# A fused convolution and two feed-forward layers: hand-made semaphores and fixed buffers in place of the framework's

## The chip, the cores and the metric

The kernel runs on one core of a Trainium2 chip. The metric is device microseconds of one execution. The core has five engines that each take their instructions from a queue of their own, in order: TensorE (PE, whose weight loads are shown as PEld), VectorE (DVE), ScalarE (ACT), GpSimd (POOL) and SyncE (SP, which issues nearly all DMAs). They wait for one another through semaphores.

## The reference, cut to what matters

```python
def reference(x, weight, w_in1, w_out1, w_in2, w_out2, a, b):      # x: 2 x 4096 x 192, float32
    w = softmax(weight, axis=-1)                                    # 8 heads x 7 taps
    x = causal_depthwise_conv(x, w)                                 # each head's 24 channels share 7 taps
    x = x.reshape(8192, 192)
    h = x @ w_in1                                                   # 192 -> 2048
    x = (h * clip(h + 3, 0, 6) / 6) @ w_out1                        # 2048 -> 192
    h = x @ w_in2
    P = a[0] + a[1] * h + a[2] * h**2 + a[3] * h**3
    Q = 1 + abs(b[0]) * abs(h) + abs(b[1]) * h**2
    return (P / (Q + 1e-6)) @ w_out2
```

## The kernel before, in words

The 8192 tokens are cut into 16 blocks of 512 (the last one into two units of 256 each, so 17 units). Every unit goes through both layers in 16 steps of 128 hidden channels (8 double steps for a half unit). Each float32 product is made of products of rounded parts: a value is split into a high part (ACT: `hi1`, `hi2`) and the rest (POOL: `lo1`, `lo2`). So one step of a layer costs TensorE five matmuls into a PSUM bank (`mm1`, `mm3`; line 504) and five into two accumulators (`product_out`, lines 518 to 523). Twenty matmuls of 512 columns make one step of both layers.

Between the matmuls of layer 2 a value goes along a chain through all the other engines (class `L2`, lines 610 to 704): ACT `A`, `t1` and `S` read the bank; DVE `t2` (line 656) and `t3` (line 668) build the numerator in the tile T; POOL `q` (line 662) the denominator in S; ACT `R` and `RR` (line 677) write the inverse square into the bank; DVE `w` (line 682) reads S and the bank and writes S; DVE `p2` (line 686) reads T and the bank and writes the bank; DVE `G` (line 691) reads S and the bank and writes T; then come `hi2`, `lo2` and the matmuls. Layer 1 is shorter: ACT `u` (line 562), DVE `g` (line 567), `hi1`, `lo1`.

At the start, 12 `warm` matmuls run on zeros, POOL clears six half tiles (`zero_low`, line 467), DVE makes the softmax of the taps in 18 tiny operations on 8 partitions (`band_ops`, lines 266 to 281), whose result `line` goes to DRAM and comes back as the convolution's band matrix (lines 952, 287), and the weights, which arrive as 64-bit words, are decoded in tiles (`mag_w`, `bound_w`, `bits_w`, `hi_w`, `lo_w`, lines 347 to 410).

The order of the work is written by the kernel itself. `Issue.at` (line 84) records every operation with a planned time, an engine, a duration, the function that emits it, and the keys that it reads and writes (`r`, `w`). `Issue.graph` (line 88) turns the keys into edges, each with a flag `end`: true if the later operation must wait for the earlier one's end, false if it only has to be issued after it. Keys need not be real buffers: `zero_low` reads the key `("line", 0)` (line 949), which the softmax operations write (line 951), though the two touch no common memory. A ring (`rings`, line 221) says how many buffers a key's name has. `Issue.order` (line 126) simulates the five engines with these edges and gives one list. The list is then emitted under the framework's manual schedule (line 967), and the framework, which sees the buffers of every single instruction, allocates the buffers of the pools and inserts all semaphore waits and signals itself. The two lines in the graph that matter here:

```python
        pred[written[key]] = True                                   # 113: reads or rewrites what p wrote
        pred[p] = pred.get(p, False) or ops[p][2] != eng            # 116: overwrites what p read
```

So if an operation overwrites what an earlier one on the same engine read (`p2` the bank that `w` read), the flag is false.

Of the kernel before, what the change touches and what calls it, by code (L numbers as in the profile page):

```python
# [62 lines left out]

class Issue:
# [23 lines left out]
    def graph(self):  # L88
        ops = sorted(self.ops, key=lambda o: o[:2])
        succ = [[] for _ in ops]  # L90
        need = [0] * len(ops)
        users, written, read, turn, gone = {}, {}, {}, {}, set()
        for k, (_, _, eng, ns, _, _, r, w, _, _) in enumerate(ops):
            pred = {}
            assert all(key in written for key in r), r
            for key in (*r, *w):
                assert key not in gone, key
                ring = self.rings.get(key[0])
                if key not in users:
# [21 lines left out]
            for p, end in pred.items():  # L121
                succ[p].append((k, end))
                need[k] += 1
        return ops, succ, need

    def order(self):
# [29 lines left out]
        while best:  # L156
# [4 lines left out]
            out.append((f, args))  # L161
# [17 lines left out]


@with_exitstack
def conv_moe_moe_kernel(ctx: ExitStack, tc: tile.TileContext, x, weight, w_in1, w_out1, w_in2, w_out2,
# [7 lines left out]
    nc = tc.nc  # L190
# [17 lines left out]
    p1 = ctx.enter_context(tc.tile_pool(name="p1", bufs=2))  # L208
    p2 = ctx.enter_context(tc.tile_pool(name="p2", bufs=2))
    xp = ctx.enter_context(tc.tile_pool(name="xp", bufs=3))  # L210
    xt = ctx.enter_context(tc.tile_pool(name="xt", bufs=3))
    xs = ctx.enter_context(tc.tile_pool(name="xs", bufs=1))
    sg = ctx.enter_context(tc.tile_pool(name="sg", bufs=4))
    sgm = ctx.enter_context(tc.tile_pool(name="sgm", bufs=5))
    xl = ctx.enter_context(tc.tile_pool(name="xl", bufs=2))
# [3 lines left out]
    bank = [ps.tile([128, C], F32, name=f"bank{k}") for k in range(4)]  # L219

# [31 lines left out]
    def warm():  # L252

        if not spare:
            spare.append(pa.tile([128, C], F32, tag="acc11", name="warm"))
# [63 lines left out]
    def load_w(kind, l, c):  # L319
# [3 lines left out]
        t = sg.tile([128, 512 * words], I32, tag="raw", name="raw")  # L323
# [17 lines left out]
    def mag_w(key, k):  # L341
# [4 lines left out]
        r[2] = sgm.tile([128, 512], F32, tag="m", name="m")[:, 0:n] if boxed(key) else r[3]  # L346
# [72 lines left out]
    def zero_x(b):  # L419
        xn[b] = xl.tile([128, NS, DM], F32, tag="xn", name="xn")  # L420
        nc.vector.memset(xn[b][0:KT - 1, 0, :], 0.0)

    def load_x(b):
# [3 lines left out]
        if b not in xn:  # L427
            xn[b] = xl.tile([128, NS, DM], F32, tag="xn", name="xn")
# [19 lines left out]
    def conv_ev(b, half):  # L448
        if b not in x1n:
            x1n[b] = xs.tile([SEG, NS, DM], F32, tag="x1n", name="x1n")  # L450
# [18 lines left out]
    def x1_hi(b, part):  # L469

        tag = "x1b" if part else "x1ah"
        if (b, tag) not in x1:
            x1[b, tag] = xp.tile([128, C], F32R, tag=tag, name=tag)
# [3 lines left out]
    def x1_lo(b, part):  # L477
        c = x1p[b, part]
        if part == 0:
            x1[b, "x1al"] = t = xp.tile([128, C], F32R, tag="x1al", name="x1al")  # L480
# [25 lines left out]
    def product_out(l, u, i, lo):  # L506

        n = units[u][2]
        if (l, u) not in acc:
            k = 1 if l or u == 1 else 0  # L510
            acc[l, u] = [pa.tile([128, C], F32, tag=f"acc{k}{j}", name=f"acc{l}{j}")[:, 0:n] for j in range(2)]
# [13 lines left out]
    def site1(b, i):  # L525

        if b == 1:
            return p2, ("T", "g2h", "g2l"), 1
        return p1, ("u", "g1h", "g1l"), 0
# [15 lines left out]
    def place2(b, i, j):  # L545
        tag = site2(b, i)[0][j]
        p = dict(u=p1, g1h=p1, g1l=p1, m=sgm).get(tag, p2)
        t = p.tile([128, C], F32R if tag[0] == "g" else F32, tag=tag, name=tag)
        return t.bitcast(F32R) if tag == "m" and j > 2 else t

    class L1:
        @staticmethod
        def mm1(b, i):
            h1[b, i] = bank[site1(b, i)[2]]
# [4 lines left out]
        def u(b, i):  # L559
            p, tags, _ = site1(b, i)  # L560
            v1[b, i] = p.tile([128, C], F32, tag=tags[0], name=tags[0])
# [8 lines left out]
        def hi1(b, i):  # L570
            p, tags, _ = site1(b, i)
            gh = p.tile([128, C], F32R, tag=tags[1], name=tags[1])
# [4 lines left out]
        def lo1(b, i):  # L577
            p, tags, _ = site1(b, i)
            gl = p.tile([128, C], F32R, tag=tags[2], name=tags[2])
# [3 lines left out]
    def x2_op(b, nm):  # L583
# [3 lines left out]
        if (b, tag) not in x2:  # L587
            n = units[b][2]
            x2[b, tag] = (low2[b % 3] if tag == "x2ml" else xt.tile([128, C], F32R, tag=tag, name=tag))[:, 0:n]
# [421 lines left out]
```

## Time and profile before

| what | value |
|---|---|
| median of three runs | 1277.68 us (1277.4 to 1277.82) |
| profiled execution | span 1275.4 us from the first to the last instruction |
| granted TensorE clock | 0.999 of full speed over the span |
| busy share | PE 98%, PEld 81%, DVE 89%, ACT 92%, POOL 87% |
| instructions | 18529, waits and DMA issues among them |
| DMA | 28.6 MB, most of it in the first 100 us |

The profiled execution's own time outside its span isn't shown; the median of the runs is 2.3 us above the span, and that is taken as what lies around it. A matmul's end in the records is modelled and overlaps the next one's start, so an idle time of TensorE shorter than some 0.15 us is not seen in the busy time.

### The profile page before, as it was taken

To read this page: it belongs to the slowest core of one execution; us is meant where nothing else is said; L and a number is where in the kernel's file an instruction comes from. 1 tells how busy PE (TensorE), PEld (TensorE's weight loads), DVE (VectorE), ACT (ScalarE), POOL (GpSimd) and SP (SyncE) were. 2 spreads that over 40 slices of the span, in tenths; PEclk is the share of its full clock that TensorE was granted. 3 is DMA by queue.
4 is the path that set the end of the run, shared out by engine and by line. 5 is a ranking of instruction groups with operands and counts; after the bars stand their busy time and mean duration, and the time that the engine had idled before them with its cause. 6 is when DMAs were issued, how large, how long until landed. Compare 5 with 4: busy or idle time off the path is not lost.

```text
span 1275.4 us, 18529 instructions
## 1 busy us (share of the span) xinstructions
PE 1252.6 (98%) x5952; PEld 1031.3 (81%) x5952; DVE 1139.4 (89%) x1824; ACT 1169.1 (92%) x2168; POOL 1116.0 (87%) x954
## 2 busy tenths in 40 slices
PE   8999999999999999999999999999999999999997
PEld 5667888888888888888888888888888888888886
DVE  6998889898898989889899898988988889899998
ACT  5778999999999999999999999999989999999997
POOL 3898898888989899888898898989889898899986
PEclk9999999999999999999999999999999999999999
DMA  5441000000000000000000001000010000000000
GB/s 167 145 147 38 16 1 17 12 13 17 5 15 11 13 16 13 16 2 12 16 13 16 14 1 25 5 16 13 1 29 2 9 5 1 13 1 13 1 13 13
DMA packets 60440, 28.60 MB, mean 22 GB/s; under 512 B 41276, under 2 KB 57272, under 8 KB 60344
## 3 DMA queue, kind: packets, MB, share of 16 engines
q1 hardware_dynamic: 60184, 27.28, 8.5%
q8 instruction: 46, 0.75, 0.3%
q14 instruction: 50, 0.41, 0.1%
q10 hardware_dynamic: 160, 0.16, 0.0%
HBM read 21.13 MB, written 6.30 MB: 22 GB/s over the span
## 4 chain that ended last, share of the span: by engine, by line
PE 80%; DVE 11%; ACT 5%; issue 2%; POOL 2%; DMA 0%; SPq 0%; DVEq 0%; ACTq 0%; POOLq 0%
PE bank L504 38%; PE acc L518 8%; PE acc L521 8%; PE acc L523 8%; PE acc L522 8%; PE acc L519 8%; PE bank L445 2%; DVE bank L686 1%; PE bank L460 1%; DVE u L567 1%; DVE bank L373 1%; DVE T L691 1%; DVE S L682 1%; ACT bank L677 1%; DVE T L656 1%
## 5 line engine op out<-in xcount | busy, mean ns | idle before, releaser
L580 POOL TENSOR_TENSOR g1l<-u,g1h 128x512 fp32r<-128x512 f32 x240 | 311.5, 1298 | 38.3 <-ACT g1h L574 8.2
L662 POOL TENSOR_TENSOR S<-A,S 128x512 f32<-128x512 f32 x169 | 219.2, 1297 | 43.2 <-ACT S L648 34.4
L704 POOL TENSOR_TENSOR g2l<-T,g2h 128x512 fp32r<-128x512 f32 x169 | 219.4, 1299 | 3.1 <-ACT g2h L696 3.0
L504 PE MATMUL bank<-low,B 128*128 128x512 f32 (+1 forms) x544 | 205.2, 377 | 0.0
L567 DVE SCALAR_TENSOR_TENSOR u<-u,bank 128x512 f32<-128x512 f32 x240 | 163.8, 682 | 33.2 <-ACT u L562 31.9
L574 ACT ACTIVATE g1h<-u 128x512 fp32r<-128x512 f32 x240 | 152.1, 634 | 3.6 <-DVE u L567 3.2
L562 ACT ACTIVATE u<-bank 128x512 f32<-128x512 f32 x240 | 143.9, 600 | 8.1 <-PE bank L504 4.0
L682 DVE SCALAR_TENSOR_TENSOR S<-S,bank 128x512 f32<-128x512 f32 x169 | 115.3, 682 | 32.1 <-ACT bank L677 26.9
L662 POOL TENSOR_TENSOR ST<-m,ST 128x512 f32<-128x512 f32 x85 | 110.3, 1298 | 26.6 <-ACT ST L648 20.6
L656 DVE SCALAR_TENSOR_TENSOR T<-T,coef,bank 128x512 f32<-128x512 f32 x169 | 125.2, 741 | 7.8 <-ACT T L641 7.0
L668 DVE SCALAR_TENSOR_TENSOR T<-T,coef,bank 128x512 f32<-128x512 f32 x169 | 125.4, 742 | 1.7
L686 DVE SCALAR_TENSOR_TENSOR bank<-T,coef,bank 128x512 f32<-128x512 f32 x169 | 126.3, 747 | 0.0
L504 PEld LDWEIGHTS bank<-low,B 128*128 128x128 f32 x544 | 102.3, 188 | 19.2
L696 ACT ACTIVATE g2h<-T 128x512 fp32r<-128x512 f32 x169 | 107.4, 635 | 10.8 <-DVE T L691 7.3
L641 ACT ACTIVATE T<-bank,coef 128x512 f32<-128x512 f32 x169 | 116.0, 686 | 0.5 <-POOL g2l L704 0.2
L691 DVE SCALAR_TENSOR_TENSOR T<-S,bank 128x512 f32<-128x512 f32 x169 | 114.9, 680 | 1.5
L673 ACT ACTIVATE A<-S 128x512 f32<-128x512 f32 x169 | 107.3, 635 | 8.8 <-POOL S L662 8.2
L504 PE MATMUL bank<-x1ah,Ah 128*128 128x512 f32 (+1 forms) x272 | 106.8, 393 | 6.4 <-DVE u L567 3.0
L704 POOL TENSOR_TENSOR m<-ST,m 128x512 fp32r<-128x512 f32 x85 | 110.3, 1298 | 1.8 <-ACT m L696 1.8
L504 PE MATMUL bank<-x2ah,Ah 128*128 128x512 f32 (+1 forms) x272 | 104.5, 384 | 3.8 <-DVE T L691 2.2
L677 ACT ACTIVATE bank<-A 128x512 f32<-128x512 f32 x169 | 102.7, 608 | 1.4 <-DVE T L668 0.4
L504 PE MATMUL bank<-x2m,B 128*128 128x512 f32 (+1 forms) x272 | 102.7, 378 | 0.6 <-ACT x2m L598 0.6
(161 smaller groups left out, 3886.1 us busy)
## 6 DMA issues: line engine op xcount, KB each, us to landing
raw<-in_moe_w_out_dram SPq DMA_DIRECT2D x16, 384.0 KB, 3.2
xn<-in_x_dram SPq DMA_DIRECT2D x14, 384.0 KB, 3.5
raw<-in_moe_w_in_dram SPq DMA_DIRECT2D x16, 256.0 KB, 3.0
out_dram<-oac SPq DMA_DIRECT2D x60, 64.0 KB, 2.0
raw<-in_moe_w_in_dram SPq DMA_DIRECT2D x16, 128.0 KB, 3.5
out_dram<-osb SPq DMA_DIRECT2D x15, 128.0 KB, 2.0
xn<-in_x_dram SPq DMA_DIRECT2D x16, 96.0 KB, 3.3
xn<-in_x_dram SPq DMA_DIRECT2D x2, 288.0 KB, 6.5
```

The costliest lines, as they stand in the source:

```text
L504: nc.tensor.matmul(out=dst[:, cs], lhsT=w[nm][:, fs], rhs=m, start=(k == 0), stop=(k == 4))
L562: act(out=v1[b, i], in_=h1[b, i], func=ACTF.Relu, scale=1.0 / 6.0, bias=0.5)
L567: stt(out=t, in0=t, scalar=1.0, in1=h1.pop((b, i)), op0=ALU.min, op1=ALU.mult)
L574: act(out=gh, in_=v1[b, i], func=ACTF.Copy)
L580: nc.gpsimd.tensor_tensor(out=gl, in0=v1.pop((b, i)), in1=f32(g1[b, i][0]), op=ALU.subtract)
L656: stt(out=d["T"], in0=d["T"], scalar=coef[:, 2:3], in1=h2[b, i], op0=ALU.add, op1=ALU.mult)
L662: (nc.gpsimd if k else nc.vector).tensor_tensor(out=d["S"], in0=d["A"], in1=d["S"], op=ALU.add if k == 1 else ALU.mult)
L668: stt(out=d["T"], in0=d["T"], scalar=coef[:, 1:2], in1=h2[b, i], op0=ALU.add, op1=ALU.mult)
L682: stt(out=d["S"], in0=d["S"], scalar=c1, in1=h2[b, i], op0=ALU.add, op1=ALU.mult)
L686: stt(out=h2[b, i], in0=v2[b, i]["T"], scalar=coef[:, 0:1], in1=h2[b, i], op0=ALU.add, op1=ALU.mult)
L691: stt(out=d["T"], in0=d["S"], scalar=2.0, in1=h2.pop((b, i)), op0=ALU.subtract, op1=ALU.mult)
L704: e.tensor_tensor(out=gl, in0=v2.pop((b, i))["T"], in1=f32(gh), op=ALU.subtract)
```

## The change

The operations and the planner's constants stay as they are. The framework's waits are turned off by a critical section, and the kernel makes its own. `graph` now also keeps, for every operation, the list `after` of the operations behind which it has to wait; `emit` goes through the planned list, collects for each operation the marks of the operations in `after`, and adds marks for an operation that touches a PSUM bank or accumulator after another engine did, and for some neighbours on POOL. `Signals.run` drops the marks that the engine is known to have seen already, directly or through another engine's signal, puts the last wait that is left on the operation's first instruction and the others into wait instructions of their own, and lets the operation's last instruction add one to its engine's semaphore. A DMA operation takes the next of 24 lanes. `Slots` gives fixed buffers, by turns. At the end `close` lets SP wait for all lanes.

```diff
+class Slots:
+    def __init__(self, pool, **tags):
+        self.line = {tag: [pool.tile(shape, dt, name=f"{tag}_{k}") for k in range(n)] for tag, (n, shape, dt) in tags.items()}
+        self.turn = dict.fromkeys(self.line, 0)
...
+class Signals:
+    def __init__(self, tc, core, lanes):
+        self.engine = dict(P=core.tensor, A=core.scalar, V=core.vector, G=core.gpsimd, S=core.sync)
+        self.sem = {e: tc.alloc_semaphore(f"done{e}") for e in "PAVG"}
+        self.sem.update({k: tc.alloc_semaphore(f"lane{k}") for k in range(lanes)})
...
+    def waits(self, e, marks):
+        want = {}
+        for sem, n in marks:
+            if self.known[e].get(sem, 0) < n:
+                want[sem] = max(n, want.get(sem, 0))
+        out = [(s, n) for s, n in want.items()
+               if not any(t != s and self.seen[t, m].get(s, 0) >= n for t, m in want.items())]
...
+    def run(self, e, dma, marks, f, args, made, signal):
...
+        todo = self.waits(e, marks)
+        f_ = lambda: f(*args)
+        keep = todo[-1:] if f.__name__ not in self.EMPTY else []
+        for s, n in todo[:len(todo) - len(keep)]:
+            self.engine[e].wait_ge(self.sem[s], n)
+        f_()
+        for s, n in keep:
+            made[0]._wait_ge(self.sem[s], n)
...
+        elif signal:
+            made[-1].then_inc(self.sem[e], 1)
+            self.count[e] += 1
+            mark = e, self.count[e]
...
+    def close(self):
+        for lane in range(self.lanes):
+            if self.known["S"].get(lane, 0) < self.count[lane]:
+                self.engine["S"].wait_ge(self.sem[lane], self.count[lane])
...
     def graph(self):
+        self.after = after = [[] for _ in ops]
+        cross = lambda p, k: ops[p][2] != ops[k][2] or ops[p][8] is not None
...
                             for p in users[line[-ring]]:
-                                pred[p] = pred.get(p, False) or ops[p][2] != eng
+                                pred[p] = pred.get(p) or cross(p, k)
                             gone.add(line[-ring])
                         if line:
-                            pred.setdefault(users[line[-1]][0], False)
+                            pred.setdefault(users[line[-1]][0], None)
...
             for key in w:
                 for p in read.pop(key, ()):
-                    pred[p] = pred.get(p, False) or ops[p][2] != eng
+                    pred[p] = pred.get(p) or cross(p, k)
...
             for p, end in pred.items():
+                if end is not None:
+                    after[k].append(p)
...
+    def emit(self, tc, core, made):
+        out = self.order()
...
+        self.signals = signals = Signals(tc, core, 24)
+        inner = lambda p, k: ops[p][2] == ops[k][2] == "P"
+        wanted = {p for k, line in enumerate(self.after) for p in line if not inner(p, k)}
...
+        held = {}
+        for k in out:
+            e = ops[k][2]
+            for key in (*ops[k][6], *ops[k][7]):
+                if key[0][:4] == "bank" or key[0][:3] == "acc":
+                    line = held.setdefault(key[0], {})
+                    for x, p in line.items():
+                        if x != e and p != k:
+                            self.after[k].append(p)
+                            wanted.add(p)
+                    line[e] = k
+        for k in out:
+            _, _, e, _, f, args, _, _, after, _ = ops[k]
+            marks = [mark[p] for p in self.after[k] if not inner(p, k) and mark[p]]
+            mark[k] = signals.run(e, after is not None and f.__name__ != "x1_raw", marks, f, args, made, k in wanted)
+        signals.close()
...
-    with tc.manual_schedule():
-        for f, a in plan.order():
-            f(*a)
+    with tc.tile_critical():
+        plan.emit(tc, core, nc.made)
```

The rest of the diff replaces every `pool.tile(...)` by the matching `slots.tile(...)`, with the same number of buffers.

## Rows read from the trace of the kernel before

**Rows 1.** Busy time by stretch: start:end, length, each engine's busy us, clock, DMA share, GB/s.
```profile
0.00:50.00 50.00, 44.46 (x179) 29.52 (x179) 38.50 (x90) 30.49 (x64) 28.87 (x36) 1.00 0.57 165
50.00:100.00 50.00, 46.85 (x205) 35.05 (x205) 47.40 (x99) 39.44 (x85) 45.05 (x45) 1.00 0.49 146
...
400.00:800.00 400.00, 399.88 (x1838) 330.84 (x1837) 358.74 (x553) 377.36 (x693) 356.77 (x299) 1.00 0.06 13
```

**Rows 2.** The chain of waits from 150 to 1200 us, shares by line.
```profile
by line: PE bank L504 44.6%; PE acc L518 8.9%; PE acc L521 8.9%; PE acc L519 8.8%; PE acc L523 8.8%; PE acc L522 8.8%; PE bank L445 2.0%; PE bank L460 1.2%; DVE bank L686 0.8%; DVE T L691 0.6%; DVE T L656 0.6%; issue 0.6%; DVE S L682 0.6%; 
```

**Rows 3.** Timeline of the start, 0 to 30 us: start us, us, engine, line, operation.
```profile
1.31 2.91 POOL L467 MEMSET low<- 64x512 f32 x6
2.21 0.15 DVE L266 TENSOR_REDUCE one<-tap 8x1 f32<-8x7 f32 x1 [0.89 <-DMA tap<-in_weight_dram]
6.21 0.22 DVE L281 TENSOR_SCALAR line<-tmp,one 8x7 f32<-8x7 f32 x1
6.91 0.70 DVE L352 TENSOR_SCALAR bank<-bank 128x512 f32<-128x512 f32 x1 [0.48 <-ACT bank L347]
7.64 0.70 DVE L370 TENSOR_SCALAR bank<-bank 128x512 int32<-128x512 int32 x1
10.88 0.92 SPq L287 DMA_DIRECT2D band<-line_d  x2
14.79 2.04 PE L445 MATMUL bank<-xn,band 128*122 128x120 f32 x16 [0.97 <-DVE bank L373]
```

**Rows 4.** DVE's timeline: the first and last of 217 neighbours L682, L686.
```profile
121.72 0.68 DVE L682 SCALAR_TENSOR_TENSOR S<-S,bank 128x512 f32<-128x512 f32 x1
122.32 0.75 DVE L686 SCALAR_TENSOR_TENSOR bank<-T,coef,bank 128x512 f32<-128x512 f32 x1
...
1266.43 0.69 DVE L682 SCALAR_TENSOR_TENSOR u<-u,bank 128x512 f32<-128x512 f32 x1
1267.04 0.75 DVE L686 SCALAR_TENSOR_TENSOR bank<-u,coef,bank 128x512 f32<-128x512 f32 x1
```

**Rows 5.** What DVE waited for: us in total, times, longest us.
```profile
DVE u L567 <- ACT u L562: 31.9, 64, 1.0
DVE S L682 <- ACT bank L677: 26.9, 48, 1.3
...
DVE ST L682 <- ACT bank L677: 14.6, 35, 1.2
```

**Rows 6.** PE and DVE at an accumulator's reuse, 351.5 to 353.2 us.
```profile
351.96 0.69 DVE L602 TENSOR_TENSOR low<-acc,low 64x512 fp32r<-64x512 f32 x1
352.01 0.39 PE L521 MATMUL acc<-g1h,O 128*128 128x512 f32 x1
...
352.80 0.47 PE L523 MATMUL acc<-g1h,O 128*128 128x512 f32 x1 [0.17 <-DVE low L602]
```

**Rows 7.** Separate wait instructions before line 682: count, ns min/median/max, first and last start.
```profile
L682 DVEq EVENT_SEMAPHORE  x104: 21/21/21, 121.4 to 1266.4; - x104
```

**Rows 8.** ACT L677 and the DVE L682 that waits for it, twice.
```profile
245.74 0.60 ACT L677 ACTIVATE bank<-m 128x512 f32<-128x512 f32 x1
...
246.45 0.69 DVE L682 SCALAR_TENSOR_TENSOR ST<-ST,bank 128x512 f32<-128x512 f32 x1 [0.81 <-ACT bank L677]
...
605.92 0.59 ACT L677 ACTIVATE bank<-m 128x512 f32<-128x512 f32 x1
...
606.54 0.69 DVE L682 SCALAR_TENSOR_TENSOR ST<-ST,bank 128x512 f32<-128x512 f32 x1 [0.48 <-ACT bank L677]
```

**Rows 9.** Who waited for DVE's L691 and L567: us in total, times.
```profile
  PEld bank L504: 7.5, 16
...
  PEld bank L504: 14.6, 26
```

**Rows 10.** SP's own waits, at the end of the kernel (L1006).
```profile
SPq L1006 <- DMA out_dram<-osb: 1.5, 1, 1.5
...
SPq L1006 <- PEq L1006: 0.6, 2, 0.4
```

More of the change, by code (lines that the diff above doesn't have):

```diff
@@ L61, with __init__, __getattr__, call @@
 )
+class Engine:
+    def __init__(self, engine, made):
+        self.engine, self.made = engine, made
+    def __getattr__(self, name):
+        f = getattr(self.engine, name)
+        def call(*args, **kw):
+            i = f(*args, **kw)
+            self.made.append(i)
+            return i
+        return call
+class Recorder:
+    def __init__(self, core):
+        self.made = []
+        for name in ("tensor", "vector", "scalar", "gpsimd", "sync"):
+            setattr(self, name, Engine(getattr(core, name), self.made))
@@ L160, in order @@
             _, _, _, ns, f, args, _, _, after, _ = ops[k]
-            out.append((f, args))
+            out.append(k)
             free[e] = start + ns
@@ L178, in order @@
         return out
+    def emit(self, tc, core, made):
+        out = self.order()
+        ops = sorted(self.ops, key=lambda o: o[:2])
+        self.signals = signals = Signals(tc, core, 24)
+        mark = {}
+        inner = lambda p, k: ops[p][2] == ops[k][2] == "P"
+        wanted = {p for k, line in enumerate(self.after) for p in line if not inner(p, k)}
+        odd = lambda k: ops[k][4].__name__ == "zero_low" or ops[k][4].__name__ == "lo_w" and ops[k][5][-1] > 0
+        pool = [k for k in out if ops[k][2] == "G"]
+        for p, k in zip(pool, pool[1:]):
+            if odd(p) != odd(k):
+                self.after[k].append(p)
[8 more added lines that the diff above has]
+                        if x != e and p != k:
+                            self.after[k].append(p)
+                            wanted.add(p)
+                    line[e] = k
[4 more added lines that the diff above has]
+        signals.close()
 @with_exitstack
@@ L345, in mag_w @@
         r.append(bank[k][:, 0:n])
-        r[2] = sgm.tile([128, 512], F32, tag="m", name="m")[:, 0:n] if boxed(key) else r[3]
+        r[2] = slots.tile("m")[:, 0:n] if boxed(key) else r[3]
         act(out=r[2] if CLAMP[side_of(key)] else r[3], in_=f32(t.rearrange("p (n w) -> p n w", w=2)[:, :, 1]), func=ACTF.Abs)
@@ L510, in product_out @@
             k = 1 if l or u == 1 else 0
-            acc[l, u] = [pa.tile([128, C], F32, tag=f"acc{k}{j}", name=f"acc{l}{j}")[:, 0:n] for j in range(2)]
+            acc[l, u] = [slots.tile(f"acc{k}{j}")[:, 0:n] for j in range(2)]
         a, c = acc[l, u]
@@ L546, in place2 @@
         tag = site2(b, i)[0][j]
-        p = dict(u=p1, g1h=p1, g1l=p1, m=sgm).get(tag, p2)
-        t = p.tile([128, C], F32R if tag[0] == "g" else F32, tag=tag, name=tag)
-        return t.bitcast(F32R) if tag == "m" and j > 2 else t
+        t = slots.tile(tag)
+        return mround[(slots.turn[tag] - 1) % 5] if tag == "m" and j > 2 else t
     class L1:
@@ L553, in mm1 @@
         def mm1(b, i):
-            h1[b, i] = bank[site1(b, i)[2]]
+            h1[b, i] = bank[site1(b, i)[1]]
             bl, c0, n = units[b]
@@ L588, in x2_op @@
             n = units[b][2]
-            x2[b, tag] = (low2[b % 3] if tag == "x2ml" else xt.tile([128, C], F32R, tag=tag, name=tag))[:, 0:n]
+            x2[b, tag] = (low2[b % 3] if tag == "x2ml" else slots.tile(tag))[:, 0:n]
         t = x2[b, tag]
@@ L759, in out_cp @@
     def out_cp(b, half):
-        osb[b, half] = sgm.tile([128, C], F32, tag="m", name="osb")[:, 0:2 * DM]
+        osb[b, half] = slots.tile("m")[:, 0:2 * DM]
         act(out=osb[b, half], in_=op_.pop((b, half))[:, 0:2 * DM], func=ACTF.Copy)
@@ L819, in transient @@
             key = (tag, ("free", k))
-            at(t, "P", ns, mm, lambda: pa.tile([128, C], F32, tag=tag, name="fb"), *args, r=r, w=[key], kind=kind)
+            at(t, "P", ns, mm, lambda: slots.tile(tag), *args, r=r, w=[key], kind=kind)
         else:
```

97 lines of the change are left out of this document (69 added, 28 removed).

## The prediction

> **What bounds the kernel now.** I read the stretches first. From 400 to 800 us TensorE is busy 399.88 of 400 us, DVE 358.74 and ACT 377.36: the steady part is bound by matmuls, and every other engine has some slack. In the first 100 us it isn't: TensorE is busy 44.46 and 46.85 of 50, DVE 38.50 and then 47.40, because DVE decodes the weights there [rows 1]. The chain of waits from 150 to 1200 us agrees: nearly all of it is matmuls, but it does pass through DVE, with 0.8% on L686 and 0.6% each on L691 and L682 [rows 2]. A wait that goes away on ACT or POOL can therefore give back little, and what makes DVE later can cost something.
>
> **The change, part by part.** The sum is made against the profiled span of 1275.4 us, with the 2.3 us around it that lead to the median of 1277.7.
>
> *A planner's edge becomes a wait, at the start.* `zero_low` reads the key of `line`, and the softmax operations write it. So far that was order only. In `graph` the flag is true (POOL against DVE), so `after` holds it, and the first softmax operation now waits for the last of the six memsets. It started at 2.21 us; the memsets run to 1.31 + 2.91 = 4.22 [rows 3]. It starts 2.0 us later. Behind it on DVE are the other softmax operations, which ended at 6.21 + 0.22 = 6.43 and will end near 8.45; then L352, which started at 6.91 and can't before 8.5, so the decoding of the first weights is 1.6 us later. `line` also goes to DRAM and back (the band loads issue at 10.88), and the convolution at 14.79 waits for both [rows 3]: 1.6 to 2.0 us. DVE has 11.5 us idle in the first 50 us, 2.6 in the next [rows 1], which could swallow it; but the chain of the first block doesn't use that idle time. Bounds 0 and 2.0; I take **+1.8**.
>
> *`p2` has to wait for `w`.* This is the largest term. `p2` overwrites the bank that `w` read, both on DVE. The flag is false, and the planner goes on treating it as mere order. But `after` leaves out only None, so false is in, and `inner` excuses TensorE alone. `w`'s mark isn't known to DVE when `p2` comes: the only other waits of `p2` are for `t3` and `RR`, which are earlier. So DVE waits for its own semaphore. Before, L686 started 0.60 us after L682, although that ran 0.68 [rows 4]: the two overlapped by 0.08. What a DVE operation pays behind one whose result it needs is seen at the start: L352 takes 0.70 and L370 starts 0.73 after it [rows 3], 0.03 past its end. So L686 will start 0.68 + 0.03 = 0.71 after L682, 0.11 later, in each of the 217 places where the two are neighbours (of 256 steps): 23.9 us more on DVE.
>
> How much of that reaches TensorE no row shows. From above: all 23.9. From below: the pieces of L682 and L686 on the chain now. 0.6% of 1050 us is 6.3 us, or some 10 pieces of L682 of 0.6, each 0.11 longer: 1.1 us. In between: DVE has on average 41 us idle in 400 [rows 1], and where it stops for ACT a delay can vanish. It stops before L567 64 times and before L682 48 + 35 times [rows 5]; in 256 − 147 = 109 steps (43%) it doesn't, and the 0.11 is handed on, toward the release of the bank by L691 and L567, for which TensorE does wait [rows 9]. Some of that meets slack at TensorE. I take a third of 23.9, nearer to the 43% than to the chain of today, which will shift as DVE gets later: **+8.0**.
>
> *The Trainium skill speaks against this term.* "VectorE: DVE Perf Modes", section "The DRAIN you can't avoid", says that the next operation does not start before the pipe is empty and that a semaphore after each costs nothing extra. By it this term would be 0, and the first rival below would come true. The overlap in [rows 4] is what makes me hold the other way.
>
> *Waits move to an operation's first instruction.* The framework let each matmul wait for what it needs alone. At 352.01 us L521 and L522 of a unit's first output product ran while DVE's L602 still read the other accumulator (351.96 + 0.69 = 352.65), and L523 alone waited, until 352.80 [rows 6]. Now L521 has to wait, and the two matmuls ahead of the wait (352.01 to 352.46) come after it: some 0.45 us. This can happen once a unit, 17 times at most, 7.7 us; where L602 was done in time it costs 0. It takes a late L602, and the matching waits of TensorE are few; I count two or three places: **+1.0**, bounds 0 and 7.7.
>
> *Waits that go away.* A wait instruction of its own in front of an operation costs when it is the one that ends last. L682 started 0.03 us after ACT's L677 ended at 605.92 + 0.59 = 606.51, but 0.11 after it ended at 245.74 + 0.60 = 246.34 [rows 8]; I put the 0.08 down to one of the 104 separate wait instructions at that line [rows 7]. TensorE's loads were seen to wait 16 + 26 times for L691 and L567 [rows 9]; if each had one such delay upstream, 42 x 0.08 = 3.4 us would come back, and nothing if none. Waits dropped elsewhere end early and are covered by the operation that runs meanwhile. Since 104 of 256 carry one at L682, and not all of these go, I take a third: **−1.1**. More signals than before are sent by TensorE's last matmuls; I cost them at nothing, because the matmuls' pace there shows no difference, and have no cover to name beyond that.
>
> *Entry, lanes, exit.* A critical section may add a round among the engines at its start and end. The two rounds at the end of the kernel cost SP 0.6 us together [rows 10]. `close` makes SP wait for up to 24 lanes one by one, part of them while the last store flies (1.5 us [rows 10]). Bounds 0 and some 2 us; I take **+0.7**. SP's DMAs stay in their order; a load of x that now waits for its block's memset is issued many steps ahead of its use, and costs nothing unless that lead is gone.
>
> Sum: 1.8 + 8.0 + 1.0 − 1.1 + 0.7 = +10.4, so 1277.7 + 10.4 = **1288.1 us**.
>
> **The rivals.** First, *the wait on DVE's own semaphore is hidden*, by DVE's slack or because it is free: without the 8.0 it is 1280.1. For it speak DVE's idle 10% [rows 1]; against it that L691 and L567 are what TensorE waits for. Second, on the other side, *the separate wait instructions were the hidden cost*: the 3.4 us come back in full, and `p2` and the first block's delay are swallowed: 1277.7 − 3.4 + 0.7 = 1275.0. It decides if TensorE's waits for DVE all hang on such an instruction and the added 0.11 on none. Against it: the start has no cover, and the 0.11 lies on the same chain. Third, *DVE's delay comes through in full*: 1.8 + 23.9 + 1.0 − 1.1 + 0.7 = +26.3, so 1304.0. Against it: DVE would still be idle some 8% of the steady part. Fourth, *the marks know more than I read*, and no new wait is made: 1277.7 − 1.1 + 0.7 = 1277.3.
>
> **How the numbers follow.** Forecast, with a tenth to a half of the 23.9 coming through and the bounds of the small terms (1282 to 1295): 0.60. First rival (1278 to 1282): 0.14. Second: 0.09. Third (1295 to 1304): 0.11. Fourth: 0.06. The range 1277 to 1297 leaves out the second and most of the third: just under 0.2. No change means within 0.2%, 1275.1 to 1280.2, about what a measurement can tell. Faster is most of the second, 0.08; within 0.2%, the fourth, half of the first and the rest of the second, 0.14; slower, all else, 0.78.
>
> **What would show it.** In the new trace L686 starts 0.7 us after L682 where they are neighbours; the first softmax operation starts after 4.2 us and the convolution near 16.6; TensorE's waits for L691 and L567 grow, spread over the whole steady part, not in one place; the separate wait instructions become fewer. If L686 still starts 0.60 after L682 the main term is gone. If it starts at 0.71 and TensorE's waits don't grow, the slack has covered it. If the time lies above 1297, DVE has become a bound, and its idle time before L567 and L682 will have gone.

## The result, and the profile after

The changed kernel takes **1286.23 us** (median of 5 runs, 1285.57 to 1287.13) against 1277.82 (1277.4 to 1278.8) for the kernel before in the same comparison: ratio 1.0066, 95% interval 1.0054 to 1.0078, or 8.4 us more. The forecast was 1288.1 in a range of 1277 to 1297. Its sum came out near, but two of its terms were too large (`p2` and the start), and a cause of over 2 us was not in it at all.

In the changed kernel all operations go through one helper, so nearly all lines are L73 and are told apart by their tiles. The head of the profile page, and its chain of work that ended last:

```profile
span 1283.8 us, 17784 instructions
PE 1258.0 (98%) x5952; PEld 1028.5 (80%) x5952; DVE 1156.1 (90%) x1824; ACT 1171.6 (91%) x2168; POOL 1116.8 (87%) x954
...
PE 80%; DVE 14%; ACT 4%; issue 1%; POOL 1%; DVEq 0%; POOLq 0%; ACTq 0%; SPq 0%
```

The span is 8.4 us longer and has 745 instructions fewer. Busy time by stretch, which answers to [rows 1]:

```profile
0.00:50.00 50.00, 45.12 (x179) 29.74 (x179) 37.87 (x90) 30.66 (x64) 28.77 (x36) 1.00 0.56 165
...
400.00:800.00 400.00, 399.81 (x1827) 328.38 (x1826) 362.49 (x550) 375.37 (x688) 355.16 (x298) 1.00 0.06 12
```

The number to look at is the count of matmuls. TensorE is as busy from 400 to 800 us as before, but starts 1827 matmuls there instead of 1838. A matmul's end is modelled, so what slows TensorE by a few hundredths of a microsecond shows in the count, not in the busy share. DVE is busier by 3.75 us in the same stretch. In the first 50 us nothing is lost. The loss accrues steadily after that: set beside the same matmul of before, TensorE was 0.15 us behind at 100 us, 1.9 at 400, 4.2 at 800 and 6.7 at 1200.

The first and the last of the 217 places where `w` and `p2` are neighbours on DVE, as in [rows 4]:

```profile
121.78 0.68 DVE L73 SCALAR_TENSOR_TENSOR S<-S,bank 128x512 f32<-128x512 f32 x1
122.49 0.75 DVE L73 SCALAR_TENSOR_TENSOR bank<-T,coef,bank 128x512 f32<-128x512 f32 x1
...
1273.70 0.68 DVE L73 SCALAR_TENSOR_TENSOR u<-u,bank 128x512 f32<-128x512 f32 x1
1274.41 0.75 DVE L73 SCALAR_TENSOR_TENSOR bank<-u,coef,bank 128x512 f32<-128x512 f32 x1
```

`p2` now starts 0.71 us after `w`, where it was 0.60: the wait is there. Over all 217 places the median went from 598 to 716 ns, 25.4 us in sum. The start, as in [rows 3]:

```profile
1.53 2.82 POOL L73 MEMSET low<- 64x512 f32 x6
4.38 0.15 DVE L73 TENSOR_REDUCE one<-tap 8x1 f32<-8x7 f32 x1 [2.85 <-POOL low L73]
7.97 1.41 DVE L73 TENSOR_SCALAR bank<-bank 128x512 f32<-128x512 f32 x2
8.07 0.30 SPq L73 DMA_DIRECT2D line_d<-line  x1
10.30 0.92 SPq L73 DMA_DIRECT2D band<-line_d  x2
14.56 1.93 PE L73 MATMUL bank<-xn,band 128*122 128x120 f32 x16
```

The softmax operations do wait for the six memsets (the trace says so: 2.85 us idle, released by POOL's `low`), 2.2 us later than before. Yet the band loads are issued at 10.30 where it was 10.88, and the convolution starts at 14.56 where it was 14.79.

How long TensorE's weight loads waited for what `G` and `g` write into T, u and the tile that is called ST before and `raw` now (us in total, times, longest), which answers to [rows 9]:

```profile
PEld bank L73 <- DVE T L73: 12.4, 23, 1.1
PEld bank L73 <- DVE u L73: 9.9, 21, 1.4
...
PEld bank L73 <- DVE raw L73: 3.0, 8, 0.7
```

Together 25.3 us in 52 places. In [rows 9], where the same waits are sorted by `G` and `g` instead of by tile, it was 7.5 + 14.6 = 22.1 us in 42. What DVE itself waited for, as in [rows 5]:

```profile
DVE u L73 <- ACT u L73: 26.1, 59, 1.0
DVE S L73 <- ACT bank L73: 25.3, 41, 1.2
...
DVE raw L73 <- ACT bank L73: 9.8, 19, 1.2
```

Together 61.2 us, where it was 31.9 + 26.9 + 14.6 = 73.4. The separate wait instructions, all at one line now (count, ns, first and last start), answer to [rows 7]:

```profile
L139 ACTq EVENT_SEMAPHORE  x530: 17/17/38, 28.2 to 1272.9; - x177
L139 POOLq EVENT_SEMAPHORE  x154: 17/17/17, 35.7 to 1250.6; - x154
...
L139 DVEq EVENT_SEMAPHORE  x7: 21/21/21, 2.3 to 92.1; - x7
```

On DVE, where 104 stood in front of `w` alone, seven are left.

### The profile page after: what moved, and what is told of

Read it like the earlier page. It is cut to its first block, busy times and chain, and to the rows that moved or that the text cites. A ratio compares the mean times of both kernels' runs of the same rounds, so it can differ in the third digit from the quotient of the medians.

```text
span 1283.8 us, 17784 instructions
## 1 busy us (share of the span) xinstructions
PE 1258.0 (98%) x5952; PEld 1028.5 (80%) x5952; DVE 1156.1 (90%) x1824; ACT 1171.6 (91%) x2168; POOL 1116.8 (87%) x954
## 4 chain that ended last, share of the span: by engine, by line
PE 80%; DVE 14%; ACT 4%; issue 1%; POOL 1%; DVEq 0%; POOLq 0%; ACTq 0%; SPq 0%
PE bank L73 42%; PE acc L73 38%; DVE bank L73 4%; DVE T L73 3%; DVE raw L73 2%; DVE u L73 1%; DVE S L73 1%; DVE low L73 1%; ACT bank L73 1%; ACT A L73 0%; ACT u L73 0%; DVE m L73 0%; ACT m L73 0%; DVE B L73 0%; ACT g1h L73 0%
## 5 line engine op out<-in xcount | busy, mean ns | idle before, releaser
L73 POOL TENSOR_TENSOR g1l<-u,g1h 128x512 fp32r<-128x512 f32 x241 | 313.0, 1299 | 41.7 <-PE acc L73 21.6
L73 DVE SCALAR_TENSOR_TENSOR T<-T,coef,bank 128x512 f32<-128x512 f32 x338 | 250.4, 742 | 8.8 <-ACT T L73 6.5
L73 POOL TENSOR_TENSOR S<-A,S 128x512 f32<-128x512 f32 x169 | 219.2, 1297 | 44.7 <-ACT S L73 37.7
L73 POOL TENSOR_TENSOR g2l<-T,g2h 128x512 fp32r<-128x512 f32 x185 | 239.8, 1297 | 3.6 <-ACT g2h L73 3.4
L73 PE MATMUL acc<-g1h,O 128*128 128x512 f32 (+1 forms) x780 | 208.3, 379 | 1.1 <-DVE low L73 1.1
L73 PE MATMUL bank<-low,B 128*128 128x512 f32 (+1 forms) x544 | 205.3, 377 | 0.0
L73 DVE SCALAR_TENSOR_TENSOR u<-u,bank 128x512 f32<-128x512 f32 x244 | 166.4, 682 | 27.3 <-ACT u L73 26.1
L73 PE MATMUL acc<-g2h,O 128*128 128x512 f32 (+1 forms) x582 | 158.1, 382 | 2.0 <-ACT g2h L73 1.9
L73 PEld LDWEIGHTS acc<-g1h,O 128*128 128x128 f32 x780 | 138.0, 188 | 27.2 <-DVE low L73 2.3
L73 ACT ACTIVATE g1h<-u 128x512 fp32r<-128x512 f32 x242 | 153.1, 633 | 5.4 <-DVE u L73 4.5
L73 PE MATMUL acc<-g1l,O 128*128 128x512 f32 (+1 forms) x520 | 150.9, 377 | 0.3 <-POOL g1l L73 0.3
L73 ACT ACTIVATE u<-bank 128x512 f32<-128x512 f32 x240 | 143.2, 597 | 7.1 <-PE bank L73 4.3
L73 DVE SCALAR_TENSOR_TENSOR S<-S,bank 128x512 f32<-128x512 f32 x169 | 115.2, 682 | 26.8 <-ACT bank L73 25.3
L73 POOL TENSOR_TENSOR raw<-m,raw 128x512 f32<-128x512 f32 x85 | 110.3, 1297 | 27.5 <-ACT raw L73 23.9
L73 DVE SCALAR_TENSOR_TENSOR bank<-T,coef,bank 128x512 f32<-128x512 f32 x169 | 127.4, 754 | 5.2
L73 ACT ACTIVATE g2h<-T 128x512 fp32r<-128x512 f32 x185 | 117.1, 633 | 14.1 <-DVE T L73 13.4
L73 DVE SCALAR_TENSOR_TENSOR raw<-raw,coef,bank 128x512 f32<-128x512 f32 x170 | 126.1, 742 | 2.4 <-ACT raw L73 1.4
L73 DVE SCALAR_TENSOR_TENSOR raw<-raw,bank 128x512 f32<-128x512 f32 x170 | 115.8, 681 | 12.3 <-ACT bank L73 9.8
L73 PEld LDWEIGHTS acc<-g2h,O 128*128 128x128 f32 x582 | 105.0, 188 | 23.2 <-ACT g2h L73 3.1
L73 PEld LDWEIGHTS bank<-low,B 128*128 128x128 f32 x544 | 102.3, 188 | 19.5
L73 PE MATMUL acc<-mr,O 128*128 128x512 f32 (+1 forms) x450 | 116.7, 384 | 1.0 <-POOL mr L73 1.0
L73 PE MATMUL acc<-g2l,O 128*128 128x512 f32 (+1 forms) x388 | 115.7, 383 | 1.8 <-POOL g2l L73 1.6
```

The source lines that it names most:

```text
L73: i = f(*args, **kw)
```

## The experiments

Times are medians, each beside runs of the kernel before on the same chip. Those of before were 1278.24 beside e1 to e4, 1277.86 beside e5 to e8, 1277.45 beside e9, e10 and e8b, and 1277.99 (a single execution) beside e11. A gain can so be counted in two ways, against the changed kernel's 1286.23 or with each time set against its own runs of before; where the two differ, both are given.

**e1: `p2` no longer waits for `w`.**

```diff
+            free = {p for p in self.after[k] if (ops[p][4].__name__, f.__name__) == ("w", "p2") and ops[p][5] == args}
-            marks = [mark[p] for p in self.after[k] if not inner(p, k) and mark[p]]
+            marks = [mark[p] for p in self.after[k] if not inner(p, k) and p not in free and mark[p]]
```

> The changed kernel with one thing taken out: p2 no longer waits on VectorE's own semaphore for w, all else as in the changed kernel. My theory (this wait, some 0.12 us in each of 217 places, a third of which reaches TensorE, is nearly the whole of the loss): p2 starts 0.60 us after w again, and the time falls by 6 to 8 us to 1278.5 to 1280. Rival A (the waits of a whole operation at its first instruction, or TensorE's waits in general, are the loss): p2 starts at 0.60 but the time stays within 2 us of 1286.2. Rival B (the wait was only one part, and the dropped wait instructions give something back): below 1277.

Measured: 1281.75 us (1280.73 to 1285.43, 7 runs), ratio to before 1.0033 (1.0022 to 1.0045). The pair on DVE, and the steady stretch:

```profile
121.80 0.68 DVE L73 SCALAR_TENSOR_TENSOR S<-S,bank 128x512 f32<-128x512 f32 x1
122.40 0.75 DVE L73 SCALAR_TENSOR_TENSOR bank<-T,coef,bank 128x512 f32<-128x512 f32 x1
```

```profile
400.00:800.00 400.00, 400.00 (x1831) 329.50 (x1830) 357.44 (x551) 376.24 (x691) 355.78 (x299) 1.00 0.06 13
```

The pair is back at 0.60 and DVE's busy time back at that of before, but only some 4.9 of the 8.4 us came back (8.4 less the 3.5 that e1 is above its own runs of before): neither theory's number. TensorE starts 1831 matmuls in the stretch, still 7 short of 1838. So the wait is a cause. What it did to the other engines shows beside the changed kernel, from which e1 differs in this wait alone. TensorE's weight loads wait 19.6 us in 40 places for T, u and `raw`, where it was 25.3 in 52, and DVE waits 34.8 + 29.8 + 12.9 = 77.5 us for ACT, where it was 61.2:

```profile
PEld bank L73 <- DVE T L73: 9.2, 18, 1.1
PEld bank L73 <- DVE u L73: 9.0, 19, 1.4
...
PEld bank L73 <- DVE raw L73: 1.4, 3, 0.5
```

```profile
DVE u L73 <- ACT u L73: 34.8, 69, 1.0
DVE S L73 <- ACT bank L73: 29.8, 52, 1.2
...
DVE raw L73 <- ACT bank L73: 12.9, 28, 1.2
```

There is a second cause of some 3 us, also spread over the run. I looked for it in the distance from each matmul's start to the next. It is 227 ns in the median in every trace, but its mean (over the distances of 215 to 245 ns after 100 us) was 227.4 before, 228.3 in the changed kernel and 228.3 in e1. Split by what the matmul reads, the excess is at one kind: matmuls of 512 columns that read an `m` buffer were followed by the next after 233.4 ns on average, all others after 227.4 to 228.9 (those above 228 are raised by matmuls close behind an `m` block). Before, those of `m` took 227.6 like the rest: the first of five, and the matmul behind the fifth, 1.13 us later:

```profile
604.51 0.39 PE L521 MATMUL acc<-m,O 128*128 128x512 f32 x1
...
605.64 0.39 PE L518 MATMUL acc<-g1l,O 128*128 128x512 f32 x1
```

Five of them in the changed kernel, and the next matmul:

```profile
510.95 1.33 PE L73 MATMUL acc<-mr,O 128*128 128x512 f32 x5
512.11 0.85 PE L73 MATMUL acc<-g2h,O 128*128 128x512 f32 x3
```

5 in 1.16 us (`mr` is the trace's name for an `m` buffer in the type that matmuls read). The change moved these buffers: before, they came from a pool at 211392 bytes and up in each partition; in the changed kernel they are allocated apart, and land at 2176. (This part of the diff is not in the excerpt above, and "replaces every `pool.tile(...)` by the matching `slots.tile(...)`" doesn't say it: the five `m` buffers get `alloc_sbuf_tensor` and a second set of names on the same memory.)

**e2: no wait of the softmax for the memsets.**

```diff
+        for k, line in enumerate(self.after):
+            if ops[k][2] == "V":
+                line[:] = [p for p in line if ops[p][4].__name__ != "zero_low"]
```

> The changed kernel without the wait of the softmax operations for the six memsets. By the prediction's first term the time falls by 1.8 us to 1284.4. By what the trace of the changed kernel shows (the convolution was not later in spite of it, because the band's transfer landed sooner) it stays within 0.6 us of 1286.2, with the softmax operations starting near 2.2 us again.

Measured: 1286.0 us (1285.92 to 1289.89), ratio 1.0069 (1.0056 to 1.0081), so 0.2 us below the changed kernel, or 0.6 with each against its own runs of before: the wait was swallowed, as the second expectation said. The trace shows where:

```profile
2.34 0.15 DVE L73 TENSOR_REDUCE one<-tap 8x1 f32<-8x7 f32 x1 [0.81 <-DMA tap<-in_weight_dram]
6.87 0.30 SPq L73 DMA_DIRECT2D line_d<-line  x1
7.74 1.43 DVE L73 TENSOR_SCALAR bank<-bank 128x512 f32<-128x512 f32 x2 [0.90 <-ACT bank L73]
10.99 0.92 SPq L73 DMA_DIRECT2D band<-line_d  x2
```

`line` leaves 1.2 us earlier than in the changed kernel, and the band loads are issued 0.7 us later. What lies between is the trip of `line` to DRAM: 4.1 us here and 2.2 there. Before it was 4.4, from this store to the band loads at 10.88 [rows 3]:

```profile
6.46 0.30 SPq L952 DMA_DIRECT2D line_d<-line  x1
```

And DVE's decoding starts only 0.23 us earlier than in the changed kernel, because it then has to wait for ACT's first result. Why the trip is longer when it starts earlier stays open; other weight transfers are in flight at the time.

**e3: TensorE's waits at the matmul that needs them.** The marks of `product_out`'s second accumulator go to its first matmul there, those of `mm1` and `mm3` by what each of the five reads:

```diff
+        first = dict(x1al=2, x2al=2, x1b=3, x1bg=3, x2m1=3, x2m1g=3, x1bl=4, x2ml=4, x2mc=4, low=4)
...
+                for p in {p for p in self.after[k] if not inner(p, k) and mark[p]}:
+                    later.setdefault(place(p, k), []).append(mark[p])
```

> The changed kernel with TensorE's waits put back to the matmul that needs them: the second accumulator's at its first matmul, those for the inputs of mm1 and mm3 at the third, fourth or fifth. By the prediction's third term 1.0 us comes back: 1285.2. If such waits never end last: 1286.2 within 0.6. If they and not the wait of p2 are the loss: 1279 to 1281.

Measured: 1285.64 us (1285.47 to 1286.17), ratio 1.0060 (1.0047 to 1.0072). That is 0.6 below the changed kernel's 1286.23, and 1.0 if each is set against its own runs of before. It doesn't decide: 1285.64 also lies within the 0.6 of the expectation that such waits never end last, and the runs overlap with the changed kernel's (1285.57 to 1287.13). The mechanism is in the traces. At the accumulators TensorE's weight loads wait for DVE's `low` (us in total, times, longest), in the changed kernel and in e3 (where the helper's line is L78):

```profile
PEld acc L73 <- DVE low L73: 2.3, 3, 1.0
```

```profile
PEld acc L78 <- DVE low L78: 1.0, 2, 0.5
```

Three places, as the forecast had counted; how much of the 1.3 us between them reaches the time isn't shown.

**e4: the suspected cost a second time.** `t3` waits for the `G` in front of it, on DVE's own semaphore:

```diff
+        vec = [k for k in out if ops[k][2] == "V"]
+        for p, k in zip(vec, vec[1:]):
+            if ops[p][4].__name__ == "G" and ops[k][4].__name__ == "t3":
+                self.after[k].append(p)
+                wanted.add(p)
```

> The changed kernel with the suspected cost added in a second place: where t3 follows G directly on VectorE (133 places, 0.598 us apart until now), it also waits for G's signal, on the semaphore on which it waits anyway, so no instruction is added. My theory: they come to be some 0.71 apart, 133 x 0.118 = 15.7 us more on VectorE, and with the share of the first 25 us that reached TensorE (0.3) 4.6 us more: 1290.8 (1288 to 1294). Rival A (VectorE's delay is not what TensorE feels): within 1 us of 1286.2. Rival B (VectorE has no slack left and it comes through in full): 1302.

Measured: 1290.99 us (1290.84 to 1291.29, 4 runs), ratio 1.0101 (1.0087 to 1.0115), as expected. One of the 133 places, `G` and `t3`:

```profile
305.22 0.68 DVE L73 SCALAR_TENSOR_TENSOR raw<-raw,bank 128x512 f32<-128x512 f32 x1
305.94 0.75 DVE L73 SCALAR_TENSOR_TENSOR T<-T,coef,bank 128x512 f32<-128x512 f32 x1
```

0.72 us apart; over all the places the median went from 598 to 716 ns, 15.8 us in sum, of which 4.8 reached the time (0.30), or 4.3 (0.27) with each against its own runs of before. DVE has slack, but it does not take in such delays whole.

**e5: the `m` buffers at the upper end of SBUF**, all waits as in the changed kernel (an unused tile of the pool keeps the place free):

```diff
-    slots.line["m"] = [core.alloc_sbuf_tensor(f"m{k}", *full)[:] for k in range(5)]
-    base = core.sbuf_base - 5 * 4 * C
+    st.tile([128, 5 * C], F32, name="hold")
+    base = 219072
+    slots.line["m"] = [core.alloc_sbuf_tensor_at(f"m{k}", *full, offset=base + k * 4 * C)[:] for k in range(5)]
...
```

> The changed kernel with its five m buffers at the upper end of SBUF (219072 bytes from the start of each partition), where the kernel before had them nearly (211392), instead of at the lower end (2176); all waits as in the changed kernel. In the changed kernel's trace a matmul of 512 columns that reads an m buffer is followed by the next after 233.4 ns, one that reads another buffer after 227.6, and in the trace of before it was 227.6 for all: 450 matmuls x 5.9 ns = 2.6 us, plus up to 0.9 us at their neighbours. Theory that the place costs it: these matmuls come at 227.6 and the time falls by 2.5 to 3.5 us to 1283 to 1283.7. Rival (something else about these buffers, as the two names on one memory or their waits): 233 stays and so does the time, 1286.2 within 0.6.

Measured: 1284.16 us (1283.9 to 1284.85), ratio 1.0051 (1.0039 to 1.0064): 2.1 us less than the changed kernel, a little short of the range. The five matmuls of above, now 1.13 us, and the steady stretch:

```profile
510.50 1.30 PE L73 MATMUL acc<-mr,O 128*128 128x512 f32 x5
511.63 0.84 PE L73 MATMUL acc<-g2h,O 128*128 128x512 f32 x3
```

The mean distance after a matmul that reads `m` is 227.7 ns, and over all matmuls 227.5, as before. Where the buffers lie is what cost. The matmuls still carry the changed kernel's more numerous signals, and none of that shows in their distance.

**e6: other buffers at the lower end.** As e5, with the two `g2l` buffers at 2176 and 4224:

```diff
...
+    slots.line["g2l"] = [core.alloc_sbuf_tensor(f"g2l{k}", *fullr)[:] for k in range(2)]
```

> As e5_m_moved, but with the two g2l buffers at the lower end of SBUF (2176 and 4224) instead. If the place decides, the matmuls that read g2l now come at 233 and those that read m at 227.6. If it is something about the m buffers, g2l stays at 227.5 there. One look; the span should then be some 388 x 5.9 ns = 2.3 us above that of e5_m_moved if the place decides, else the same within 0.6.

Measured in one execution: 1289.88 us. The matmuls that read `g2l` now come at 233.4 ns and those of `m` at 227.6: the place decides, not which buffer it is. GpSimd, which writes `g2l`, is slower there too (mean ns of one, in e6):

```profile
L73 POOL TENSOR_TENSOR g2l<-T,g2h 128x512 fp32r<-128x512 f32 x185 | 244.3, 1321 | 3.5 <-ACT g2h L73 3.3
```

It was 1299 in e5. The time is 5.7 above e5, not 2.3, but 3.1 of that is lost in one place, at 40 us, on a DVE operation on 128 x 1 numbers. DVE and GpSimd in e6:

```profile
39.56 3.01 DVE L73 TENSOR_TENSOR root<-root,inv 128x1 f32<-128x1 f32 x1
```

```profile
37.63 2.58 POOL L73 TENSOR_TENSOR g2l<-T,g2h 128x512 fp32r<-128x512 f32 x2
40.17 1.15 POOL L73 TENSOR_TENSOR O<-m,O 128x256 fp32r<-128x256 f32 x2
41.29 1.27 POOL L73 TENSOR_TENSOR g1l<-u,g1h 128x512 fp32r<-128x512 f32 x1
```

It ends at 42.57, when GpSimd's run of operations ends (41.29 + 1.27 = 42.56). In e5:

```profile
39.61 0.61 DVE L73 TENSOR_TENSOR root<-root,inv 128x1 f32<-128x1 f32 x1
```

```profile
37.66 2.53 POOL L73 TENSOR_TENSOR g2l<-T,g2h 128x512 fp32r<-128x512 f32 x2
40.16 1.16 POOL L73 TENSOR_TENSOR O<-m,O 128x256 fp32r<-128x256 f32 x2
```

There it got in between two operations of GpSimd, at 37.66 + 2.53 = 40.19, and ended at 40.22. From 60 us to the end TensorE falls back by 2.4 us against e5, as the place should cost.

**e7: e1 and e5 together.**

> The changed kernel without the wait of p2 for w (as e1_no_w_wait) and with the m buffers at the upper end (as e5_m_moved). If the two are separate and together nearly the whole loss, the gains add: 1281.75 - 3.0 = 1278.8 (1278.2 to 1279.5), within 0.2% of the kernel before. If a third cause of the same size is left, it stays above 1280.5.

Measured: 1278.75 us (1277.95 to 1279.87, 11 runs), ratio 1.0006 (0.9997 to 1.0015), as expected. Steady stretch:

```profile
400.00:800.00 400.00, 399.97 (x1837) 330.56 (x1836) 358.53 (x553) 377.46 (x693) 356.92 (x300) 1.00 0.06 13
```

1837 matmuls against 1838 before: the steady part is that of before again. The two causes are separate, add up, and leave 0.9 us, which the interval doesn't tell from nothing. Beside e5, on the same chip, the wait of `p2` is worth 1284.16 - 1278.75 = 5.4 us; beside the changed kernel it was 4.9.

**e8: e7 with e2 and e3 as well.**

> As e7_both, with the softmax wait taken out (e2) and TensorE's waits at the matmul that needs them (e3) too. By the single runs these two give 0.2 and 0.6 us: 1278.0 (1277.2 to 1279). If the dropped wait instructions were worth the 1.1 us of the prediction's fourth term and nothing but the entry and exit is left against it, it comes out at or just below the kernel before: 1277.5. If the prediction's first term is real once the other causes are gone, 1.8 us less than e7_both: 1277.

Measured: 1278.44 us (1277.52 to 1279.48, 11 runs), ratio 1.0006 (0.9997 to 1.0014), in the expected range and 0.3 below e7, which the runs don't tell apart. The first term doesn't come to life when the other causes are gone.

**e9: the five `m` buffers spread over SBUF.**

```diff
+    place = [2176, 12992, 31424, 66240, 117440]
+    slots.line["m"] = [core.alloc_sbuf_tensor_at(f"m{k}", *full, offset=place[k])[:] for k in range(5)]
...
```

> The changed kernel with its five m buffers at five places of SBUF instead of side by side at the lower end: m0 at 2176, m1 at 12992, m2 at 31424, m3 at 66240, m4 at 117440 bytes. This maps how far the slow place reaches: where a matmul that reads the buffer is followed by the next after 233 ns the place is slow, at 227.6 it isn't. If only the lowest few KB are slow (where coef and the constants that other engines read also lie), m0 and perhaps m1 show 233 and the rest 227.6; if it grows with the distance from some point, there are values in between. The time should be between e5_m_moved and the changed kernel: 1284.2 to 1286.2.

Measured in one execution: 1285.15 us, in the expected range. Mean distance after a matmul that reads them: 233.6 ns at 2176, then 227.4, 228.2, 227.6 and 228.0. Only the lowest is slow.

**e10: the last signal on the operation itself.**

```diff
-        todo = self.waits(e, marks)
+        todo = sorted(self.waits(e, marks), key=lambda m: self.made.get(m, 0))
...
```

> As e8_all_four, but where an operation waits for several semaphores, the signal that is sent last in the program's order stands on the operation itself and the earlier ones on the wait instructions in front of it (so far the order of the graph's edges decided). By the prediction's fourth term a wait that ends last on a separate instruction costs 0.08 us more than on the operation: some of the 530 separate waits of ScalarE and 160 of GpSimd are such, and TensorE would feel a part, 0.5 to 1.5 us: 1277 to 1278. If the separate waits cost nothing that reaches TensorE: 1278.4 within 0.4.

> e8_all_four once more, beside e10_late_last on the same chip, so that the two can be compared: 1278.4 within 0.5.

Measured: e10 1277.08 us (1276.66 to 1277.69), ratio 0.9997 (0.9988 to 1.0006); e8b 1277.72 (1276.95 to 1277.92), ratio 1.0000 (0.9991 to 1.0009), 11 runs each. e8b came out 0.2 below its range; the kernel before, too, was 0.4 lower here than beside e8. The 0.6 us between e10 and e8b are at the lower end of what was expected, and the two sets of runs overlap. e10 is the fastest version that I ran, and it can't be told from the kernel before.

**e11: the `m` buffers a little higher, with `u` below them.**

```diff
+    slots.line["u"] = [core.alloc_sbuf_tensor(f"u{k}", *full)[:] for k in range(2)]
...
```

> The changed kernel with the two u buffers at the lower end of SBUF (2176 and 4224) and the five m buffers behind them at 6272, 8320, 10368, 12416 and 14464. Until now matmuls that read m were slow at 2176 to 10368 (233 ns to the next) and not at 12992. If the place alone decides and its border lies near 12.7 KB, m0 to m2 show 233, m3 something in between or 227.6, and m4 227.6; if what decides is which buffers lie lowest, all five are at 227.6, since now u, which no matmul reads, is lowest. One look at where the border is; the time should be between e5_m_moved and the changed kernel, 1284.2 to 1286.2, if the operations on u don't mind the place (u by ScalarE 597 ns, by VectorE 682 ns, g1l by GpSimd 1299 ns until now), and above if they do.

Measured in one execution: 1289.6 us, with the same loss at 40 us as in e6 (`root` 2.97 us; TensorE is 3.4 behind the changed kernel from 60 us on and 3.5 at the end, so nothing else was lost or won). All five `m` buffers come at 233.4 to 233.6 ns, the one at 12416 and the one at 14464 too, although a buffer at 12992 was at 227.4 in e9. A border in the address is refuted, and so is that the lowest buffers pay. What all runs so far leave standing is another property of the address. Every slow buffer begins at a multiple of 128 bytes (2176 = 17 x 128, and on in steps of 2048 to 14464); every fast one named here leaves 64 when divided by 128 (211392, 219072, and 12992, 31424, 66240 and 117440 of e9). No run moves a buffer by 64 bytes and nothing else. Operations on `u` by ScalarE (597 ns), VectorE (682) and GpSimd (1298) don't mind the place.

## Why the prediction was right, point by point

**The wait of `p2` for `w`** was the right mechanism, in the right place, at the right price on DVE: forecast 0.11 us in 217 places, 23.9 in all; measured 0.118 and 25.4. It was mis-sized in one factor, the share that reaches TensorE. I took a third; e1 and e7 give 4.9 and 5.4 us of 25.4, a fifth, and e4's dose 0.27 to 0.30 of 15.8. The rows of DVE's waits show where most of it went: `g` and `w` find ACT's result ready more often when DVE comes later, and between e1 and the changed kernel 77.5 - 61.2 = 16.3 us less waiting took in as much of the 25.4. What came through shows at TensorE's waits for T, u and `raw`: 25.3 - 19.6 = 5.7 us, beside 4.9 in the time. They grew as the prediction said. So +8.0 should have been +5. The Trainium skill's "VectorE: DVE Perf Modes", section "The DRAIN you can't avoid", by which a semaphore behind each operation costs nothing extra (measured there on copies), does not hold for this pair: with the wait 716 ns, without it 598 (before and in e1), and the same two numbers at the other pair in e4.

**The edge of the memsets** became a wait, as the prediction said, and was worth next to nothing: +1.8 forecast, 0.2 to 0.6 measured (e2). The step that failed is "the chain of the first block doesn't use that idle time". The trip of `line` through DRAM, which I took as a fixed length added behind it, ended near 10.3 to 11.0 us whether it began at 6.5, 6.9 or 8.1, so a wait of 2 us in front of it moved nothing behind it. The lower bound of 0 was the nearer one.

**Waits at an operation's first instruction**: +1.0 forecast, 0.6 to 1.0 measured (e3), 0.3 for this and the memsets together in e8. The waits are there, in three places as forecast; their price is too small for these runs to confirm or refute.

**Waits that go away**: -1.1 forecast; not measured by itself. e10 suggests that a term of this kind exists: moving waits from the instruction in front onto the operation was worth 0.6 us, between two sets of runs that overlap. Its size could only come from what is left over. With the other causes undone (e8, e8b) the kernel is 0.3 to 0.6 us above before, and entry and exit cost it 0.5 to 0.7 (next point), which leaves +0.1 to -0.4 for the waits that went away. The intervals of e8 and e8b are wider than that, so the term stays open.

**Entry and exit**: +0.7 forecast. The first DMA is issued at 0.91 where it was 0.72, and the last one, at 1280.34, leaves 3.46 us to the end of the span where it was 2.93 (1272.47 to 1275.4): 0.7 in all. Against it, what lies outside the span is 1.8 us in the changed kernel's runs (1285.57 - 1283.8) and 2.0 in those of before beside e1 (1276.79 - 1274.8; the 2.3 that the prediction used came from two different executions). So 0.5 to 0.7 is left. The last store before, and in the changed kernel:

```profile
1272.47 0.37 SPq L765 DMA_DIRECT2D out_dram<-osb  x1
```

```profile
1280.34 0.37 SPq L73 DMA_DIRECT2D out_dram<-m  x1
```

**What was missing** is the place of the `m` buffers: 2.1 us (e5) to 2.6 (e1 against e7, each set against its own runs of before: 3.5 - 0.9). The diff showed that they are allocated apart; I read it as a matter of names and gave it no term, since no row of before has a matmul that pays for a place. So the sum was nearer than its terms, and that is luck: 3 us too much for `p2` and 1.2 to 1.6 for the start were partly offset by 2 to 2.6 not counted. The account that the runs support: 5 for `p2`, 2.1 to 2.6 for the place, 0.9 for all the rest together, 8.4 in all.

**Of the rivals**, the fourth (no new wait) falls with the 0.71, and so does the free wait of the first; that slack hides it, and the third (in full, 1304), fall with e1; the second (faster by the dropped waits) falls with the result, and even with the losses taken out, in e8, the time is level with before, not 3 us below it.

**What stays open**: what makes a place slow. It was slow for every buffer read by matmuls that lay in front of the pool with `coef` and the other constants (2176 to 14464 in four layouts), and not for any behind `coef` (12992 and up). The very same buffers are those that begin at a multiple of 128 bytes, so the layout and the remainder by 128 are two rivals that no run separates; a run with the `m` buffers of the changed kernel 64 bytes higher and all else in its place would. Neither DVE nor GpSimd has to be at work for it: in the changed kernel the distance after a matmul that reads `m` is 233.2 ns in the 19 cases in which DVE was idle from one start to the next, and 233.5 in the 34 in which GpSimd was.

## What to carry to other kernels

When waits are made by hand, an overwrite on the same engine need not be a wait (before, `p2` started while `w` still ran on the same bank): go through such edges one by one, since each wait on the engine's own semaphore cost 0.12 us here and a fifth to a third of it came through although the engine had a tenth of its time idle. When a change also moves buffers, compare the distance between the starts of like operations by buffer, and count the operations in a steady stretch, because busy shares showed neither cause. Take the causes out one at a time and then together; here the first experiment's miss, not the forecast's near hit, showed that there was a second cause.

## What the hardware showed that I had not expected

- A matmul of 512 columns was followed by the next after 233.4 ns instead of 227.6 when its moving operand (the `m` or `g2l` buffer) lay at one of the addresses from 2176 to 14464 that are named above, all multiples of 128, and GpSimd's operation that writes such a buffer took 1307 to 1321 ns instead of 1299. That the address matters e5, e6 and e9 show; which property of it does, no run tells.
- One DVE operation on 128 x 1 numbers took 3.0 us in two traces (e6, e11) and 0.5 to 0.63 in all others: it ends when an operation of GpSimd ends, and whether it gets in at the first such end or only after the whole run of them decides over 2.4 us. What decides it stays open. The Trainium skill's "SBUF — State Buffer", section "SBUF: two separate sides", says that a DVE operation with two inputs in SBUF and a GpSimd operation that reads SBUF lock each other out for a whole instruction; this operation has two such inputs, and the traces agree, except that in e6 and e11 it was kept out for several operations of GpSimd and not one. Single executions of e1 and e2 lay 3.7 and 3.9 us above their medians; they have no trace, so that it is the same event is a guess.
- The trip of 8 KB to DRAM at the start, from its issue to that of the loads behind it, took 3.4 to 4.4 us in the traces in which it began at 6.5 to 6.9 us, and 2.2 to 2.8 in those in which it began at 8.1.
